# A q projection ahead of z, w1's low parts behind ol, and the second layer norm's sums on other engines

## The chip, the cores and the metric

The kernel runs on one core of one Trainium2 chip. The core has five engines, each with an instruction queue of its own that is worked off in order: TensorE (PE in the profile, with its weight loads as PEld), VectorE (DVE), ScalarE (ACT), GpSimd (POOL) and SyncE (SP), which here only issues transfers. They wait for each other through semaphores. Matrix products are written to PSUM, a small memory of banks; everything else on the chip lies in SBUF. The metric is the time of one execution on the device in microseconds, as the median of several runs.

## The reference

The block has 2048 tokens of 512 channels, in fp32. First comes linear attention with 32 heads of 16 channels, whose features are two softmaxes per head, of the projected logits and of their negative:

```python
pq = einsum("bhsd,hdf->bhsf", q, w_phi)          # q, k, v = layernorm(x) @ wqkv, by heads
phi_q = concat([softmax(pq), softmax(-pq)], -1)  # phi_k from k in the same way
kv = einsum("bhsf,bhsd->bhfd", phi_k, v)
z  = einsum("bhsf->bhf", phi_k)
num = einsum("bhqf,bhfd->bhqd", phi_q, kv)
den = einsum("bhqf,bhf->bhq", phi_q, z)[..., None] + 1e-6
h = x + (num / den) @ wo                          # heads side by side
u = gelu(einsum("bsd,sf->bdf", layernorm(h), w1) + b1)   # F = 1792, over the token axis
out = h + transpose(einsum("bdf,fs->bds", u, w2) + b2)
```

z is a sum over all tokens, so no den can be computed before the last k tile is done. The second layer norm needs the mean and the variance of every row of h.

## The kernel before

**Tiling.** The tokens are cut into 16 tiles of 128 rows. Every fp32 operand of a large product is split into a high part (rounded to fp32r by ScalarE, `whi`, `xs`, `oh`, `hs`) and a low part (the rest, by a subtraction on DVE or POOL, `wlo`, `ol`, `wol`). Each product is then three matmuls, high by high, high by low and low by high (`mm3`, L61 to L63). One projection of a tile is four such triples, twelve matmuls of 512 columns.

**Stages.** A first stage folds w_phi into the weights and computes k, v and the sums kv and zacc for all tiles (to some 144 us of the profile), with six of the q tiles in between. The main loop, `for it in range(NT + 3)`, follows (144 to 276 us). It carries a token tile through several iterations: iteration `it` transposes the features of tile it (`s_tr`), computes num of tile it-1 (`s_num`), the output product of tile it-2 (`s_wo`) and its h (`s_h`), and the normalised tile it-3 (`s_hn`). The first two columns of w1, `fill(0)` and `fill(1)`, are multiplied with finished tiles inside this loop. After it come the rest of w1 and gelu, and from about 340 us the products with w2, in which PE never stands still.

**What sets the order.** A planner orders the instructions by its own cost estimates. Between `ms.enter_context(tc.manual_schedule(...))`, behind the loop over the k tiles, and `ms.close()`, behind the main loop, the order on PE, DVE, ACT and POOL is that of the program text; so each of these engines' queues can be read off the code. SP's queue and everything behind `ms.close()` stay with the planner.

**q tiles.** `q_mm` issues the next q tile's projection into one of the two PSUM buffers of `ps_q` (tag `pu`), so tile n+2 needs the buffer of tile n. `q_logits` takes the per-head maximum and minimum on DVE, subtracts the maximum on DVE (L144), and, for tiles 6 and later, copies the logits on ACT (L146), after which the buffer is free; `negate` then forms the negative half on POOL (L159). `q_exp` is one exponential on ACT (L169). q tiles 6 to 9 are issued in the straight piece of text between the loop over k and the main loop; tile 10 in iteration 0, tiles 11 and 12 in iteration 1, where tile 11 follows num of tile 0, and so on to tile 15 in iteration 4. From iteration 5 on `fill(1)` uses the buffers of `ps_q`.

**z and den.** The last addition to zacc is DVE's (L481). Two products with a matrix of ones (L486) spread zacc to all rows, ACT copies the result to zB (L487), and POOL multiplies each q tile's exponentials with it (`s_ez`, L440). `s_den` reduces this on DVE (from L449, tile `tz`) to the weights W, and `s_pq` (L458) applies W on POOL. `wo_hi` and `wo_lo` (L426, L429) split wo on ACT and POOL, row block by row block. They stand in the same straight piece.

**The main loop's waits.** num and the transposes share one PSUM tile (`tn`, one buffer): the transposes of tile it wait for ol of tile it-1 (DVE, L553), which waits for oh (ACT, L548); num waits for the copies `pht` (ACT, L528). The output product has one buffer `po`, freed by `s_h`, whose addition (L568) reads it. `s_h` then computes the mean and the variance by bn_stats and bn_aggr and prepares two columns of `ve2`. `s_rstd` turns them into the scale and the shift on POOL (a power and a product). `s_hn` normalises on ACT and splits the tile on ACT and POOL (`hs`).

**w1.** `stream` loads two row blocks of one w1 column pair, ACT forms the high part and DVE the low part at once (`split`, L56 and L57). `fill_load` calls it at the end of an iteration. The first pairs are loaded in iteration 2, further ones in about every second iteration for both columns.

Of the kernel before, what the change touches and what calls it, by code (L numbers as in the profile page):

```python
# [17 lines left out]
P = 128  # L18
# [15 lines left out]
def block_kernel(ctx: ExitStack, tc: tile.TileContext, x, xT, wT, phic, wo, w1, b1, w2, b2,  # L34
# [10 lines left out]
    b1s = cst.tile([P, NF], F32, name="b1s")  # L45
    b2s = cst.tile([P, NT], F32, name="b2s")
    r1 = cst.tile([P, NT], F32, name="r1")
    mv2 = cst.tile([P, NT, 2], F32, name="mv2")
    r2 = cst.tile([P, NT], F32, name="r2")
    cst.tile([P, 56], F32, name="pad")  # L50
    nc.vector.memset(ones, 1.0)
    nc.vector.memset(mhalf, -0.5)

    def split(hi, lo, src, lo_engine):

        nc.scalar.activation(hi, src, AF.Copy)  # L56
        return lo_engine.tensor_sub(lo, src, hi)  # L57
# [97 lines left out]
    def negate():  # L155

        if MN:
            ev, mn = MN.pop(0)
            nc.gpsimd.tensor_sub(ev[:, :, 1], mn.unsqueeze(3).to_broadcast([P, NPR, 2, DH]), ev[:, :, 1])  # L159

    def run(*lists):

        for i in range(max(map(len, lists))):
            for ops in lists:
                if i < len(ops):
                    ops[i]()
# [192 lines left out]
    def q_mm():  # L359
        if q["mm"] < NT:  # L360
            PS[q["mm"]] = proj(q["mm"], wqh, wql, ps_q, "pu")
            q["mm"] += 1
# [65 lines left out]
    def wo_lo(j):  # L428
        nc.gpsimd.tensor_sub(wol[:, j], WO[j], woh[:, j])  # L429
# [27 lines left out]
    def s_pq(t):  # L457
        nc.gpsimd.tensor_mul(heads(EQ[t]), heads(EQ[t]), W[t].rearrange("p g c h -> p (g c h)").unsqueeze(2).to_broadcast([P, 2 * H, DH]))  # L458

    def lead(it, mm):  # L460

        if 0 <= it + 1 < NT:
            s_pq(it + 1)
        if 0 <= it + 3 < NT:
            s_ez(it + 3)
        negate()
        for _ in range(mm):
            q_mm()
        q_exp(0)
# [4 lines left out]
    k_norm(NT - 1, False)  # L474
    for j in range(KD):
        wo_hi(j)
    wo_lo(0)
    wo_lo(1)
    v_kv()
    run(q_logits(0))  # L480
    nc.vector.tensor_add(zacc, zacc, PK[NT - 1])  # L481
    negate()
    zB = big.tile([P, NG, P], F32, name="zB", tag="big")
    for g in range(2):
        pz = ps_k.tile([P, 4, P], F32, name="pk_ps")
# [2 lines left out]
    q_exp(0)  # L488
    s_ez(0)
    s_ez(1)  # L490
    wo_lo(2)
    wo_lo(3)
    q_mm()
    v_kv()
    run(s_den(0))
    run(q_logits(0))
# [54 lines left out]
    def s_ol(t):  # L551
        oh, ol, pn = OS[t]
        return [lambda: nc.vector.tensor_sub(ol, pn, oh)]  # L553
# [11 lines left out]
    def s_h(t):  # L565

        h = HT[t]
        nc.vector.tensor_add(h, PO.pop(t), h)  # L568
        nc.sync.dma_start(out[t * P:(t + 1) * P, :], h)
        st = ak.tile([P, 6], F32, name="st2")  # L570
        nc.vector.bn_stats(st, h)
        nc.vector.bn_aggr(mv2[:, t, :], st)
        VE[t] = ak.tile([P, 2], F32, name="ve2")
        nc.vector.tensor_scalar(VE[t][:, 0:1], mv2[:, t, 1:2], 1.0 + EPS, EPS * EPS, op0=ALU.mult, op1=ALU.add)
        nc.vector.tensor_scalar_mul(VE[t][:, 1:2], mv2[:, t, 0:1], -1.0)

    def s_rstd(t):
        nc.gpsimd.tensor_tensor(r2[:, t:t + 1], VE[t][:, 0:1], mhalf[:, :1], op=ALU.pow)
# [8 lines left out]
    w1v = w1.rearrange("(k p) f -> p k f", p=P)  # L587
    w2v = w2.rearrange("(k p) s -> p k s", p=P)

    def stream(src, k0, n, c0, w):  # L590

        raw = wf.tile([P, n, w], F32, name="wraw")
        wh_ = wf.tile([P, n, w], F32R, name="whi")
        wl_ = wf.tile([P, n, w], F32R, name="wlo")
        nc.sync.dma_start(raw, src[:, k0:k0 + n, c0:c0 + w])
        LO.append(split(wh_, wl_, raw, nc.vector).ins)
        return wh_, wl_

    PU, WI, LO = {}, {}, []
# [7 lines left out]
    def fill(p, pool=None):  # L607

        t = FN[p]
        FN[p] = t + 1  # L610
        if FL[p] <= t:
            fill_load(p)
        if t == 0:
            PU[p] = [pool.tile([P, D], F32, name="pu", tag="pu") for _ in range(2)]
        a, b = WI[p, t - t % 2]
        for c in range(2):
            mm3(PU[p][c], a[:, t % 2, c * P:(c + 1) * P], b[:, t % 2, c * P:(c + 1) * P],
                HN[t][:, 0], HN[t][:, 1], t == 0, t == NT - 1)

    for it in range(NT + 3):  # L620
        if 0 <= it < NT:
            s_x(it)
        if 0 <= it - 3 < NT:
            s_rstd(it - 3)
        if 0 <= it - 1 < NT:
            s_num(it - 1)
        if 0 <= it - 2 < NT:
            s_wo(it - 2)
        if it == 1:
            run(q_logits(0))  # L630
            q_mm()
        if 0 <= it < NT:
            s_tr(it)
        if it == 0:
            s_kv()
        lead(it, 1)
        den = s_den(it + 2) if it + 2 < NT else []
        run((s_ol(it - 1) if 0 <= it - 1 < NT else []) + q_logits(1) + (q_sums(0) if it > 0 else []), den)
        if it > 0:
            negate()  # L640
        if 0 <= it - 3 < NT:
            s_hn(it - 3)
        if 0 <= it - 2 < NT:
            s_h(it - 2)
        if FN[0] <= it - LAG:
            fill(0, ps_f)
        for _ in range(2):
            if q["logits"] == NT and FN[1] <= it - LAG:
                fill(1, ps_q)
        for p in range(2):  # L650
            if it >= LAG - 2 and FL[p] <= FN[p] + 1:
                fill_load(p)
    ms.close()
    a2.close()
    aq.close()
# [195 lines left out]
```

## Time and profile before

| | us |
|---|---|
| median of 3 runs | 536.01 (535.8 to 536.05) |
| profiled execution | 535.76 |
| its span, first to last instruction | 534.0 |
| PE busy | 522.6 |
| DVE busy | 393.5 |
| ACT busy | 258.6 |
| POOL busy | 236.6 |
| PE idle, 120 to 160 us | 1.69 |
| PE idle, 160 to 220 us | 2.26 |
| PE idle, 220 to 400 us | 0.0 |

A row of a timeline has the start of an instruction (or of several alike, merged, with their count) from the span's start, its duration, both in microseconds, its engine, its line, the operation, the tile written and the tiles read with their sizes, and in brackets how long its engine had been idle before it and what it waited for. A row of a group of instructions has the line, the engine, the shapes and the count, then the total busy time in us and the mean of one in ns, then the idle time in front of the group and what ended it. PE's matmuls overlap: each lasts longer than the distance to the next.

### The profile page before, as it was taken

How to read it: one execution, taken by the hardware profiler on the slowest of the kernel's cores; microseconds unless marked ns; L12 is line 12 of the kernel's file. 1: busy time of each engine (PE TensorE's matmuls, PEld its weight loads, DVE VectorE, ACT ScalarE, POOL GpSimd, SP SyncE). 2: the span in 40 equal slices, each digit the busy share in tenths (PEclk: the TensorE clock that was granted, in tenths of full speed). 3: DMA queues.
4: the chain of work that ended last, by engine and by line, in shares of the span. 5: the costliest groups of instructions: out<-in, count | busy, mean ns of one | idle time of the engine just before them, and what ended most of it. 6: DMA issues, size and time to landing. Idle time of an engine off the chain costs nothing.

```text
span 534.0 us, 9892 instructions
## 1 busy us (share of the span) xinstructions
PE 522.6 (98%) x3872; PEld 450.4 (84%) x3872; DVE 393.5 (74%) x722; ACT 258.6 (48%) x406; POOL 236.6 (44%) x184
## 2 busy tenths in 40 slices
PE   8999999998999999999999999999999999999995
PEld 7888888886876777778788888888899999999995
DVE  6993999875699989986536523835768878888774
ACT  6998844434346555544546423525443343343340
POOL 2589699878978989985435000000001101100110
PEclk9999999999999999999999999999999999999998
DMA  8534300021302233333256333533014556536631
GB/s 315 196 113 118 99 21 21 1 78 63 97 4 86 73 101 118 100 121 118 91 166 179 98 100 97 160 107 91 20 41 108 139 149 144 133 119 140 138 80 40
DMA packets 45486, 55.84 MB, mean 105 GB/s; under 512 B 3968, under 2 KB 33024, under 8 KB 45440
## 3 DMA queue, kind: packets, MB, share of 16 engines
q1 hardware_dynamic: 43136, 51.38, 30.2%
q0 software_dynamic: 2016, 3.67, 5.1%
q8 instruction: 30, 0.49, 0.4%
q10 hardware_dynamic: 288, 0.17, 0.1%
q14 instruction: 16, 0.13, 0.1%
HBM read 46.81 MB, written 8.39 MB: 103 GB/s over the span
## 4 chain that ended last, share of the span: by engine, by line
PE 91%; DVE 5%; ACT 2%; issue 1%; POOL 0%; DVEq 0%; POOLq 0%
PE py L745 26%; PE pu L61 12%; PE pu L62 12%; PE pu L63 12%; PE po L61 3%; PE pv L62 3%; PE pv L63 3%; PE pv L61 3%; PE pk_ps L61 2%; PE pk_ps L63 2%; PE pk_ps L62 2%; PE tn L526 2%; PE po L62 2%; PE po L63 2%; PE kvp L205 2%; PE tn L544 1%
## 5 line engine op out<-in xcount | busy, mean ns | idle before, releaser
L57 DVE TENSOR_TENSOR wlo<-wraw,whi 128x512 fp32r<-128x512 f32 (+1 forms) x84 | 100.3, 1204 | 69.4 <-ACT whi L56 67.9
L56 ACT ACTIVATE whi<-wraw 128x512 fp32r<-128x512 f32 (+1 forms) x84 | 81.9, 987 | 127.1 <-PE py L745 73.8
L783 POOL DMA_DIRECT2D out<-ot x14 | 12.5, 1001 | 211.3 <-DVE ot L781 211.3
L745 PE MATMUL py<-uf,whi 128*128 128x256 f32 x560 | 96.2, 283 | 0.0
L61 PE MATMUL pu<-hs,whi 128*128 128x512 f32 x224 | 87.6, 394 | 0.6 <-ACT eq L146 0.6
L62 PE MATMUL pu<-hs,whi 128*128 128x512 f32 x224 | 87.2, 389 | 0.0
L63 PE MATMUL pu<-hs,wlo 128*128 128x512 f32 x224 | 86.8, 389 | 0.0
L745 PEld LDWEIGHTS py<-uf,whi 128*128 128x128 f32 x560 | 83.3, 192 | 0.0
L745 PE MATMUL py<-uf,wlo 128*128 128x256 f32 x280 | 69.9, 283 | 0.0
L61 PEld LDWEIGHTS pu<-hs,whi 128*128 128x128 f32 x224 | 42.1, 188 | 9.5 <-ACT eq L146 1.1
L745 PEld LDWEIGHTS py<-uf,wlo 128*128 128x128 f32 x280 | 49.7, 192 | 0.0
L63 PEld LDWEIGHTS pu<-hs,wlo 128*128 128x128 f32 x224 | 42.0, 188 | 8.8
L62 PEld LDWEIGHTS pu<-hs,whi 128*128 128x128 f32 x224 | 42.1, 188 | 8.2
L528 ACT ACTIVATE pht<-tn 128x512 f32<-128x512 f32 x32 | 17.4, 596 | 49.7 <-PE tn L526 49.7
L440 POOL TENSOR_TENSOR ez<-eq,zB 128x1024 f32<-128x1024 f32 x16 | 38.4, 2406 | 0.7 <-ACT zB L487 0.7
L745 PE MATMUL py<-un,whi 128*128 128x256 f32 x224 | 38.4, 283 | 0.0
L193 POOL TENSOR_TENSOR pk<-pk,sk 128x1024 f32<-128x1024 f32 x16 | 31.1, 1944 | 9.4 <-DVE sk L192 7.6
L745 PEld LDWEIGHTS py<-un,whi 128*128 128x128 f32 x224 | 33.2, 192 | 0.1
L458 POOL TENSOR_TENSOR eq<-eq,w 128x1024 f32<-128x1024 f32 x16 | 31.1, 1942 | 3.1 <-DVE w L455 3.1
L197 POOL TENSOR_TENSOR zacc<-zacc,pk 128x1024 f32<-128x1024 f32 x13 | 31.3, 2409 | 0.6
L57 POOL TENSOR_TENSOR hs<-hn,hs 128x512 fp32r<-128x512 f32 x16 | 20.6, 1291 | 21.1 <-ACT hs L56 21.1
L61 PE MATMUL po<-woh,oh 128*128 128x512 f32 x64 | 26.6, 416 | 1.0 <-DVE h L568 1.0
(161 smaller groups left out, 1144.3 us busy)
## 6 DMA issues: line engine op xcount, KB each, us to landing
wraw<-in_w SPq DMA_DIRECT2D x112, 256.0 KB, 2.8
xraw<-in_xT SPq DMA_DIRECT2D x16, 256.0 KB, 3.1
xh<-in_x SPq DMA_DIRECT2D x16, 256.0 KB, 2.7
h<-in_x SPq DMA_DIRECT2D x16, 256.0 KB, 2.9
out<-h SPq DMA_DIRECT2D x16, 256.0 KB, 2.2
out<-ot POOLq DMA_DIRECT2D x14, 256.0 KB, 4.8
wraw<-in_wT SPq DMA_DIRECT2D x12, 256.0 KB, 4.9
wo<-in_wo SPq DMA_DIRECT2D x4, 256.0 KB, 3.8
```

The lines of the kernel that those rows point to most:

```text
L56: nc.scalar.activation(hi, src, AF.Copy)
L57: return lo_engine.tensor_sub(lo, src, hi)
L61: nc.tensor.matmul(o, ah, bh, start=first, stop=False)
L62: nc.tensor.matmul(o, ah, bl, start=False, stop=False)
L63: nc.tensor.matmul(o, al, bh, start=False, stop=last)
L193: nc.gpsimd.tensor_mul(heads(PK[t]), heads(PK[t]), sk.unsqueeze(2).to_broadcast([P, 2 * H, DH]))
L197: nc.gpsimd.tensor_add(zacc, zacc, PK[t])
L440: nc.gpsimd.tensor_mul(EZ[t], EQ[t], zB)
L458: nc.gpsimd.tensor_mul(heads(EQ[t]), heads(EQ[t]), W[t].rearrange("p g c h -> p (g c h)").unsqueeze(2).to_broadcast([P, 2 * H, DH]))
L528: nc.scalar.activation(PHT[t][:, half * 4:half * 4 + 4, :], ptr[:, half], AF.Copy)
L745: nc.tensor.matmul(o, a[x], b[:, y], start=start and i == 0, stop=stop and i == 2, skip_group_check=True)
L783: nc.gpsimd.dma_start(out[(t + i) * P:(t + i + 1) * P, :], flat(ot[:, i]), accum_op=ALU.add)
```

## The change

Five edits, in the order of the diff:

- The tile `mv2` goes and a column `eps2`, set once, comes. The pad behind them grows.
- In the straight piece in front of the main loop the projection of q tile 7 (`q_mm`) moves from behind zB's copies to in front of z's two products; zacc's last addition is made in two halves; of wo's four low parts one (instead of two) stands in front of zB, behind the negation of q tile 6 instead of in front of it, and three (instead of two) stand behind the first two `s_ez`.
- h's addition becomes a `scalar_tensor_tensor` that also gives the row's sum. bn_stats, bn_aggr and two small instructions on DVE go. In the next iteration ACT makes the negative mean, one pass of squares with their sum, and the variance column (`s_moments`), behind oh and in front of the `pht` copies.
- On POOL `s_pq` moves from `lead` to the front of `s_rstd`, which stood first in the iteration.
- w1's low parts are not subtracted at once: `stream` puts them on a list, and `flush` empties it behind ol of the next iteration (and at once where `fill` itself had to load).

```diff
-    mv2 = cst.tile([P, NT, 2], F32, name="mv2")
+    eps2 = cst.tile([P, 1], F32, name="eps2")
...
+    nc.vector.memset(eps2, EPS * EPS)
...
     def lead(it, mm):
-        if 0 <= it + 1 < NT:
-            s_pq(it + 1)
         if 0 <= it + 3 < NT:
             s_ez(it + 3)
...
-    wo_lo(0)
-    wo_lo(1)
     v_kv()
     run(q_logits(0))
-    nc.vector.tensor_add(zacc, zacc, PK[NT - 1])
+    for g in range(2):
+        nc.vector.tensor_add(zacc[:, 4 * g:4 * g + 4, :], zacc[:, 4 * g:4 * g + 4, :], PK[NT - 1][:, 4 * g:4 * g + 4, :])
     negate()
+    wo_lo(0)
+    q_mm()
     zB = big.tile([P, NG, P], F32, name="zB", tag="big")
...
     q_exp(0)
     s_ez(0)
     s_ez(1)
-    wo_lo(2)
-    wo_lo(3)
-    q_mm()
+    for j in range(1, KD):
+        wo_lo(j)
     v_kv()
...
     def s_h(t):
         h = HT[t]
-        nc.vector.tensor_add(h, PO.pop(t), h)
+        VE[t] = ak.tile([P, 4], F32, name="ve2", bufs=3)
+        nc.vector.scalar_tensor_tensor(h, PO.pop(t), 1.0, h, op0=ALU.mult, op1=ALU.add, accum_out=VE[t][:, 2:3])
         nc.sync.dma_start(out[t * P:(t + 1) * P, :], h)
-        st = ak.tile([P, 6], F32, name="st2")
-        nc.vector.bn_stats(st, h)
-        nc.vector.bn_aggr(mv2[:, t, :], st)
-        VE[t] = ak.tile([P, 2], F32, name="ve2")
-        nc.vector.tensor_scalar(VE[t][:, 0:1], mv2[:, t, 1:2], 1.0 + EPS, EPS * EPS, op0=ALU.mult, op1=ALU.add)
-        nc.vector.tensor_scalar_mul(VE[t][:, 1:2], mv2[:, t, 0:1], -1.0)
+
+    def s_moments(t):
+        junk = ak.tile([P, D], F32, name="hj", bufs=1)
+        nc.scalar.activation(VE[t][:, 1:2], VE[t][:, 2:3], AF.Copy, scale=-1.0 / D)
+        nc.scalar.activation(junk, HT[t], AF.Square, bias=VE[t][:, 1:2], accum_out=VE[t][:, 3:4])
+        nc.scalar.activation(VE[t][:, 0:1], VE[t][:, 3:4], AF.Identity, scale=(1.0 + EPS) / D, bias=eps2)
...
+    LATER = []
+
+    def flush():
+        while LATER:
+            wl_, raw, wh_ = LATER.pop(0)
+            LO.append(nc.vector.tensor_sub(wl_, raw, wh_).ins)
...
-        LO.append(split(wh_, wl_, raw, nc.vector).ins)
+        nc.scalar.activation(wh_, raw, AF.Copy)
+        LATER.append((wl_, raw, wh_))
...
         if FL[p] <= t:
             fill_load(p)
+            flush()
...
             s_x(it)
-        if 0 <= it - 3 < NT:
-            s_rstd(it - 3)
         if 0 <= it - 1 < NT:
             s_num(it - 1)
+        if 0 <= it - 3 < NT:
+            s_moments(it - 3)
         if 0 <= it - 2 < NT:
             s_wo(it - 2)
...
+        if 0 <= it + 1 < NT:
+            s_pq(it + 1)
+        if 0 <= it - 3 < NT:
+            s_rstd(it - 3)
         lead(it, 1)
         den = s_den(it + 2) if it + 2 < NT else []
-        run((s_ol(it - 1) if 0 <= it - 1 < NT else []) + q_logits(1) + (q_sums(0) if it > 0 else []), den)
+        run(s_ol(it - 1) if 0 <= it - 1 < NT else [])
+        flush()
+        run(q_logits(1) + (q_sums(0) if it > 0 else []), den)
...
+    flush()
     ms.close()
```

More of the change, by code (lines that the diff above doesn't have):

```diff
@@ L47, in block_kernel @@
     r1 = cst.tile([P, NT], F32, name="r1")
-    mv2 = cst.tile([P, NT, 2], F32, name="mv2")
+    eps2 = cst.tile([P, 1], F32, name="eps2")
     r2 = cst.tile([P, NT], F32, name="r2")
-    cst.tile([P, 56], F32, name="pad")
+    cst.tile([P, 80], F32, name="pad")
     nc.vector.memset(ones, 1.0)
     nc.vector.memset(mhalf, -0.5)
+    nc.vector.memset(eps2, EPS * EPS)
     def split(hi, lo, src, lo_engine):
@@ L161, in run @@
     def run(*lists):
-        for i in range(max(map(len, lists))):
+        for i in range(max(len(x) for x in lists)):
             for ops in lists:
```

## The prediction

> **What bounds the kernel now.** I read the page first, then the timeline of TensorE (PE) from 115 to 300 us for places where it stands still, then the timelines of GpSimd (POOL), ScalarE (ACT) and VectorE (DVE) around each. The page:
>
> ```profile
> span 534.0 us, 9892 instructions
> PE 522.6 (98%) x3872; PEld 450.4 (84%) x3872; DVE 393.5 (74%) x722; ACT 258.6 (48%) x406; POOL 236.6 (44%) x184
> PEclk9999999999999999999999999999999999999998
> ```
>
> PE is busy for 98% of the span, at full clock. So the change can win only where PE waits in the stretch that it edits. These rows bound that:
>
> ```profile
> 121.89 0.39 PE L61 MATMUL pv<-wvh,xs 128*128 128x512 f32 x1
> 124.39 0.39 PE L63 MATMUL pv<-wvh,xs 128*128 128x512 f32 x1
> 126.46 1.96 PE L486 MATMUL pk_ps<-zacc,ones 128*128 128x512 f32 x4 [1.69 <-DVE zacc L481]
> ...
> 148.27 0.67 PE L544 MATMUL tn<-pht,kvB 64*32 64x128 f32 x32
> 148.86 0.50 PE L61 MATMUL pu<-wqh,xs 128*128 128x512 f32 x1
> ...
> 171.71 0.50 PE L61 MATMUL po<-woh,oh 128*128 128x512 f32 x1 [1.03 <-DVE h L568]
> ...
> 186.82 0.50 PE L61 MATMUL pu<-hs,whi 128*128 128x512 f32 x1 [0.65 <-ACT eq L146]
> ...
> 200.38 1.06 PE L526 MATMUL tn<-ident,eq 128*128 128x128 f32 x8 [0.53 <-DVE ol L553]
> ```
>
> The twelve matmuls of one projection start at 121.89 and 124.39 for first and last: 2.50/11 = 0.227 us apart, though each lasts 0.39. So a wait costs its idle time plus 0.39 - 0.23 = 0.16: A, in front of z, 1.85; C, in front of an output product (iteration 4), about 1.1; D, in front of a w1 product (iteration 5), 0.81; E, in front of iteration 7's transposes, 0.69. All of it is 4.5 us, under 1%.
>
> **The q tile in front of z.** q tile 7 takes 12 x 0.227 = 2.73 us and needs nothing late. It starts at 124.39 + 0.23 = 124.62 and ends at 127.34: wait A is filled, and PE is 1.85 us ahead behind z. But z starts at 127.34 instead of 126.46, 0.88 later, and zB with it. The sum for z, in two halves, is no limit: even at its old pace it ended at 126.4. Who waits for zB is POOL:
>
> ```profile
> 129.13 4.77 POOL L440 TENSOR_TENSOR ez<-eq,zB 128x1024 f32<-128x1024 f32 x2 [0.68 <-ACT zB L487]
> 133.85 2.54 POOL L429 TENSOR_TENSOR wol<-wo,woh 128x512 fp32r<-128x512 f32 x2
> ...
> 145.85 1.08 POOL L159 TENSOR_TENSOR eq<-mn,eq 128x512 f32<-128x512 f32 x1
> 149.00 1.94 POOL L458 TENSOR_TENSOR eq<-eq,w 128x1024 f32<-128x1024 f32 x1 [2.07 <-DVE w L455]
> ```
>
> From 129.13 to 146.93 POOL runs ten instructions without a gap, the last the negation of q tile 8. The change puts one more of wo's low parts into this row (three behind the ez pair instead of two: 2.54/2 = 1.27). The time that POOL is spared in front of z is lost, as it waits there for zB. So the negation ends 0.88 + 1.27 = 2.15 us later. Behind it:
>
> ```profile
> 139.34 1.15 ACT L169 ACTIVATE eq<-eq,r 128x1024 f32<-128x1024 f32 x1 [2.74 <-POOL eq L159]
> 146.96 1.16 ACT L169 ACTIVATE eq<-eq,r 128x1024 f32<-128x1024 f32 x1 [0.23 <-POOL eq L159]
> 148.02 0.57 ACT L146 ACTIVATE eq<-pu 128x512 f32<-128x512 f32 x1
> ```
>
> The exponential of tile 8 waits for that negation already (0.23). Behind it in ACT's queue stands the copy of q tile 9's logits, ending at 148.59, which frees the PSUM buffer of q tile 11: ps_q has two, and 11 follows 9. Tile 11 started at 148.86, just behind the num product, so it had at most 0.27 to spare; wait D shows 0.05 from such a copy's end (186.77) to the product. With the copy at 148.59 + 2.15 = 150.74 tile 11 starts at 150.79: **+1.93 us against before**, with no PE work left undone or done in advance. The 1.85 is not saved; it becomes part of 1.85 + 1.93 = 3.8 us of waiting, of which some 1.3 falls ahead of the last kv product (exponential 7 waits for POOL too, 2.74 in the row above, and v's last copy queues behind it) and 2.5 ahead of tile 11. After it POOL idles again (2.07 at 149.00), so the loss stays at 1.93. Below: 1.85 less, if the chain on POOL did not hold; above: 2.15.
>
> **h's sum and squares.** DVE loses bn_stats and its three small followers and h's addition takes the fused form:
>
> ```profile
> 163.16 0.69 DVE L571 BATCH_NORM_STATS2 st<-h 128x6 f32<-128x512 f32 x1
> L568 DVE TENSOR_TENSOR h<-po,h 128x512 f32<-128x512 f32 x16 | 10.9, 684 | 6.1 <-PE po L63 6.1
> L781 DVE SCALAR_TENSOR_TENSOR ot<-py,b2s,u 128x512 f32<-128x512 f32 x7 | 5.2, 748 | 0.0
> L113 ACT ACTIVATE sqj<-xh,st 128x512 f32<-128x512 f32 x16 | 11.5, 721 | 0.3
> L113 ACT ACTIVATION_READ_ACCUMULATOR sqj<-xh,st 128x1 f32 x16 | 3.0, 191 | 0.0
> 184.16 1.09 ACT L528 ACTIVATE pht<-tn 128x512 f32<-128x512 f32 x2 [3.15 <-PE tn L526]
> ```
>
> Saved on DVE: 163.16 to 164.24 (below), 1.08 us a tile. Added: 0.06 by the fused form (748 - 684); writing out its sum is in no row, 0 to 0.19 by ACT's accumulator read; I take 0. ACT pays 0.72 + 0.19 and two instructions on one column (about 0.2 each), 1.3 us, between oh and the pht copies, where it waits 3.15 for PE: nothing. If that cover went, 1.3 an iteration. POOL's rstd, now behind pq, would wait for ACT with ez and the negation behind it; pq's 1.94 covers that.
>
> **w1's low parts behind ol.** Wait C first, in rows of ACT, DVE and POOL:
>
> ```profile
> 163.54 0.61 ACT L548 ACTIVATE oh<-tn 128x512 fp32r<-128x512 f32 x1
> 164.24 1.28 DVE L57 TENSOR_TENSOR wlo<-wraw,whi 128x512 fp32r<-128x512 f32 x2
> 165.44 0.68 DVE L553 TENSOR_TENSOR ol<-tn,oh 128x512 fp32r<-128x512 f32 x1
> 166.04 1.21 DVE L449 TENSOR_REDUCE tz<-ez 128x64 f32<-128x1024 f32 x1
> 170.97 0.68 DVE L568 TENSOR_TENSOR h<-po,h 128x512 f32<-128x512 f32 x1
> 162.70 1.06 POOL L159 TENSOR_TENSOR eq<-mn,eq 128x512 f32<-128x512 f32 x1 [1.07 <-ACT eq L146]
> 165.55 1.93 POOL L458 TENSOR_TENSOR eq<-eq,w 128x1024 f32<-128x1024 f32 x1
> ```
>
> Before: statistics, two wlo, ol, then 4.93 us from tz (166.04) to h (170.97), and PE 0.74 later. After: ol cannot use the 1.08 saved, for it waits for oh, which ACT gives behind two whi copies at 164.15. In PE's new time (+1.93): oh 166.08, ol to 166.72, two wlo at 0.6 each to 167.92, h at 172.85, PE at 173.59, against 171.71 + 1.93 = 173.64. C stays; the short wait ahead of it at 166 goes into it. But the wlo now fall on POOL's pq, moved up to 163.76 + 1.93 = 165.69 and running to 167.6. What that does:
>
> ```profile
> 179.70 1.29 POOL L57 TENSOR_TENSOR hs<-hn,hs 128x512 fp32r<-128x512 f32 x1 [0.30 <-ACT hs L56]
> 180.18 1.36 DVE L57 TENSOR_TENSOR wlo<-wraw,whi 128x512 fp32r<-128x512 f32 x1
> ```
>
> Beside POOL's subtraction wlo took 1.36 instead of 0.68 and ended 0.55 behind it (181.54 against 180.99). The same beside pq: first wlo to 168.15, second 168.75, h at 173.68, PE at 174.42: **+0.78**, with the fused form +0.84. No row has wlo beside pq (one input of which is a small broadcast), so 0 to 0.84; I take the upper end, as the hs row is the nearest. The Trainium skill (SBUF — State Buffer, section "Who interferes with whom") says that a VectorE instruction with two SBUF inputs contends with any GpSimd instruction that reads SBUF, and that the loser blocks fully; the hs row agrees. By that rule the sum has the 0.84 and D's 0.55 below; without it neither.
>
> D: q tile 15's logits copy frees the buffer.
>
> ```profile
> 180.41 0.60 ACT L548 ACTIVATE oh<-tn 128x512 fp32r<-128x512 f32 x1 [0.26 <-PE tn L544]
> 182.06 1.20 DVE L449 TENSOR_REDUCE tz<-ez 128x64 f32<-128x1024 f32 x1
> 184.60 0.68 DVE L144 TENSOR_TENSOR eq<-pu,mx 128x512 f32<-128x512 f32 x1
> 186.18 0.59 ACT L146 ACTIVATE eq<-pu 128x512 f32<-128x512 f32 x1
> ```
>
> At +2.77 (1.93 + 0.84): oh ends at 183.78, ol at 184.4; pq starts behind hs at 183.76 and holds wlo until 185.7 + 0.55 = 186.25; the shift, 3.22 behind tz's start, ends at 189.47; ACT was ready to copy at 188.95. **+0.5**, or 0 without the blocking.
>
> ```profile
> 197.66 1.98 DVE L57 TENSOR_TENSOR wlo<-wraw,whi 128x512 fp32r<-128x512 f32 x2 [0.84 <-ACT whi L56]
> ```
>
> E: ol stood behind these two (with 0.84 of waiting for whi). Now it goes as soon as oh is there: **-0.69**. Next late would be oh, ready with about 0.3 to spare. Queue SP's loads of w1 wait for wraw a little longer, four buffers deep: nothing.
>
> **Sum.** 1.93 + 0.84 + 0.5 - 0.69 = +2.6. The profiled execution took 535.76 (span 534.0), 0.25 below the median: 538.4 us; from the median 538.6; I say 538.5. Both ends of the blocking give 537.1 to 538.4.
>
> **Rivals.**
> 1. *The blocking costs nothing and DVE's relief counts* (pq leaves wlo alone, and ol comes earlier than I think). 1.93 - 0.69 = +1.2, less up to 1.1 if C also goes: 535.9 to 537.0. For it: no row shows pq against wlo. Against: C's chain starts at oh, which the change does not speed up.
> 2. *Faster: POOL does not hold PE.* If wo's three low parts run while POOL waits for zB, instead of between ez and pq, the row to the negation of tile 8 is 17.8 - 2.54 = 15.26 from 130.01, ends at 145.3, 1.7 earlier than before, and PE keeps the 1.85: -1.85 - 0.69 = -2.5, or -1.2 with the blocking: 533.2 to 534.6. It decides when that negation ends by 145.3 or so. For it: they need only woh, done long before. Against: before's POOL kept them behind the ez pair, at 133.85.
> 3. *The clock falls in the new wait.* At the kernel's start PE ran a slow stretch:
>
> ```profile
> L286 PE MATMUL pk_ps<-ones 128*128 128x128 f32 x18 | 4.2, 430 | 1.1 <-DVE mhalf L52 1.1
> ```
>
> These matmuls stand 0.23 apart (4.2/18); twice as fast they would take 2.1 less. If the wait ahead of tile 11 is long enough, the same is paid again: 540.5. For it: 3.8 us of waiting within 9. Against: A's 1.85 left the clock at 9 in every slice. The Trainium skill (TensorE: Matmul & The Clock Gate, Part 1) names an idle window of about 3.4 us; by it 2.5 us would not do and one wait of 3.8 would.
>
> **How the numbers follow.** Main case, with or without half of the blocking (537.1 to 539.2): 0.64. Rival 1: 0.16. Rival 2: 0.12. Rival 3: 0.08. A difference under 0.2% (1.07 us) can't be told from none here, so faster 0.12, same 0.15, slower 0.73. The range 535.8 to 540.3 leaves out rival 2 and the end of rival 3; the main case's own is 537.0 to 539.2.
>
> **What would show it.** Right: no idle ahead of z, z 0.9 later; exponential 8 waits some 4 us for POOL; PE waits for ACT's copy ahead of q tile 11 by some 2.5 us and for v's copy ahead of the last kv products; wlo beside pq near 1.3 us; PE straight through iteration 7; 16 statistics gone from DVE; ACT's squares ahead of pht without delaying it. Wrong: tile 11 right behind num, or a wait for ACT's moments ahead of hn on POOL and PE, or a new order in the planned parts before 115 and after 275 us, where PE has nothing to gain.

## The result and the profile after

The changed kernel takes 542.8 us (median of four runs, 542.31 to 543.4) against 535.99 us before, measured beside it: a ratio of 1.0127, 95% interval 1.0112 to 1.0142. It is slower, as forecast, but by 6.8 us and not by 2.5, and it lies above the range of 535.8 to 540.3. The profiled execution took 543.4 us, with a span of 541.6.

The page of the changed kernel:

```profile
span 541.6 us, 9889 instructions
PE 524.0 (97%) x3872; PEld 451.8 (83%) x3872; DVE 376.8 (70%) x676; ACT 277.6 (51%) x470; POOL 233.2 (43%) x184
PEclk9999999999989999999999999999999999999999
```

VectorE (DVE) has 16.7 us less to do and TensorE (PE) the same 3872 matmuls, yet the span is 7.7 us longer. One slice of the clock's row has an 8. So the time lies in new idle places of PE and in one stretch at a lower clock. These are PE's rows in the changed kernel that show a wait, with the start of q tile 6's projection (the last piece of work ahead of everything that the change touches) and the last matmul ahead of z:

```profile
119.36 0.50 PE L62 MATMUL pu<-wqh,xs 128*128 128x512 f32 x1
...
127.42 0.40 PE L64 MATMUL pu<-wqh,xs 128*128 128x512 f32 x1
127.65 0.59 PE L486 MATMUL pk_ps<-zacc,ones 128*128 128x512 f32 x1
...
143.57 0.65 PE L206 MATMUL kvp<-pk,vs 128*32 128x64 f32 x32 [1.31 <-ACT vs L185]
...
150.97 0.80 PE L62 MATMUL pu<-wqh,xs 128*128 128x512 f32 x1 [2.15 <-ACT eq L147]
...
167.27 0.50 PE L62 MATMUL po<-woh,oh 128*128 128x512 f32 x1 [0.34 <-DVE h L568]
176.27 0.50 PE L62 MATMUL po<-woh,oh 128*128 128x512 f32 x1 [1.75 <-DVE h L568]
...
191.71 0.50 PE L62 MATMUL pu<-hs,whi 128*128 128x512 f32 x1 [0.95 <-ACT eq L147]
...
210.78 0.50 PE L62 MATMUL po<-woh,oh 128*128 128x512 f32 x1 [1.84 <-DVE h L568]
...
225.93 0.50 PE L62 MATMUL po<-woh,oh 128*128 128x512 f32 x1 [0.77 <-DVE h L568]
241.07 0.50 PE L62 MATMUL po<-woh,oh 128*128 128x512 f32 x1 [0.77 <-DVE h L568]
```

In the kernel before, q tile 6 starts earlier:

```profile
119.04 0.50 PE L61 MATMUL pu<-wqh,xs 128*128 128x512 f32 x1
```

So 0.32 us of the span's 7.66 (541.62 against 533.96, first start to last end) arose ahead of the change: in other kernels below with the same first stage this start wanders between 119.0 and 119.7. I therefore count from q tile 6's start: 414.92 us before, 422.26 after, +7.34.

Where these 7.34 arise, by the start of the same matmul in both traces, less the 0.32:

| place | start before, after | lost there |
|---|---|---|
| q tile 11 waits for its PSUM buffer | 148.86, 150.97 | 1.79 |
| its first matmuls at the lower clock (to the transposes of iteration 1) | 151.72, 155.41 | 1.58 |
| output product, iteration 3 | 163.18, 167.27 | 0.40 |
| output product, iteration 4 (C) | 171.71, 176.27 | 0.47 |
| w1 product, iteration 5 (D), up to iteration 6's transposes | 192.54, 197.43 | 0.33 |
| transposes of iteration 7 (E) | 200.38, 204.58 | -0.69 |
| output product, iteration 8 | 204.75, 210.78 | 1.83 |
| output product, iteration 10 | 219.06, 225.93 | 0.84 |
| output product, iteration 12 | 233.36, 241.07 | 0.84 |

The rest, -0.05, is spread to the end. Two blocks carry the loss: q tile 11 with its clock (3.37) and the output products in iterations 8, 10 and 12 (3.51).

The chain ahead of q tile 11, on GpSimd (POOL) and ScalarE (ACT) of the changed kernel:

```profile
130.25 4.75 POOL L441 TENSOR_TENSOR ez<-eq,zB 128x1024 f32<-128x1024 f32 x2 [1.25 <-ACT zB L487]
134.96 3.80 POOL L430 TENSOR_TENSOR wol<-wo,woh 128x512 fp32r<-128x512 f32 x3
...
148.19 1.07 POOL L160 TENSOR_TENSOR eq<-mn,eq 128x512 f32<-128x512 f32 x1
149.29 1.15 ACT L170 ACTIVATE eq<-eq,r 128x1024 f32<-128x1024 f32 x1 [2.64 <-POOL eq L160]
150.34 0.57 ACT L147 ACTIVATE eq<-pu 128x512 f32<-128x512 f32 x1
```

Negation of tile 8 to 149.26, exponential, copy of tile 9's logits to 150.91, q tile 11 at 150.97: link by link the row that the prediction gave. Behind it q tile 11's matmuls start 0.43 us apart, and 0.23 apart again from 154.49 on:

```profile
151.99 0.63 PE L64 MATMUL pu<-wqh,xs 128*128 128x512 f32 x1
152.42 0.63 PE L62 MATMUL pu<-wqh,xs 128*128 128x512 f32 x1
...
154.49 0.40 PE L64 MATMUL pu<-wqh,xs 128*128 128x512 f32 x1
154.72 0.40 PE L62 MATMUL pu<-wqh,xs 128*128 128x512 f32 x1
```

The windows of the changed kernel (busy time of PE, PEld, DVE, ACT, POOL, then PE's granted clock, the share and rate of the DMA) show the same stretch as a clock of 0.96, where before it was 1.00:

```profile
115.00:160.00 45.00, 41.54 (x414) 32.51 (x414) 28.47 (x54) 17.52 (x28) 33.82 (x20) 0.96 0.23 72
```

The second block, iteration 7, on DVE and POOL of the changed kernel:

```profile
203.54 0.69 DVE L552 TENSOR_TENSOR ol<-tn,oh 128x512 fp32r<-128x512 f32 x1 [2.38 <-ACT oh L547]
204.15 2.27 DVE L596 TENSOR_TENSOR wlo<-wraw,whi 128x512 fp32r<-128x512 f32 x2
...
210.04 0.68 DVE L568 SCALAR_TENSOR_TENSOR h<-po,h 128x512 f32<-128x512 f32 x1
210.64 0.08 DVE L568 DVE_READ_ACCUMULATOR h<-po,h 128x1 f32 x1
...
203.32 1.94 POOL L459 TENSOR_TENSOR eq<-eq,w 128x1024 f32<-128x1024 f32 x1
205.22 1.00 POOL L579 TENSOR_TENSOR r<-ve,mhalf 128x1 f32<-128x1 f32 x1
```

and the same place before, DVE and then PE:

```profile
203.99 0.68 DVE L568 TENSOR_TENSOR h<-po,h 128x512 f32<-128x512 f32 x1
...
204.75 0.50 PE L61 MATMUL po<-woh,oh 128*128 128x512 f32 x1
```

Before, h ended at 204.67 and the product that needs the buffer `po` started at 204.75: there was 0.08 us to spare at most (where the product did wait, at 171.71, it started 0.06 us after h's end). After, two low parts stand between ol and h. They start at 204.15 and the next instruction starts at 206.34: 2.19 us on a chain with no slack. POOL's pq overlaps the first and its power the second; the power, 0.55 elsewhere, takes 1.00.

### The profile page after: what moved, and what is told of

Same layout as the page of the kernel before. It is cut to its first block, busy times and chain, and to the rows that moved or that the text cites. A ratio compares the mean times of both kernels' runs of the same rounds, so it can differ in the third digit from the quotient of the medians.

```text
span 541.6 us, 9889 instructions
## 1 busy us (share of the span) xinstructions
PE 524.0 (97%) x3872; PEld 451.8 (83%) x3872; DVE 376.8 (70%) x676; ACT 277.6 (51%) x470; POOL 233.2 (43%) x184
## 4 chain that ended last, share of the span: by engine, by line
PE 82%; DVE 8%; ACT 4%; POOL 3%; DMA 1%; issue 1%; SPq 0%; DVEq 0%; ACTq 0%; POOLq 0%
PE py L762 26%; PE pu L62 10%; PE pu L63 10%; PE pu L64 10%; PE pk_ps L62 2%; PE pv L63 2%; PE pk_ps L63 2%; PE pk_ps L64 2%; PE pv L64 2%; PE pv L62 2%; PE po L62 2%; DVE wlo L596 2%; PE po L63 2%; PE po L64 2%; POOL ez L441 2%; PE tn L525 2%
## 5 line engine op out<-in xcount | busy, mean ns | idle before, releaser
L57 ACT ACTIVATE whi<-wraw 128x1792 fp32r<-128x1792 f32 x28 | 47.7, 1704 | 77.9 <-PE py L762 70.5
L596 DVE TENSOR_TENSOR wlo<-wraw,whi 128x512 fp32r<-128x512 f32 x56 | 45.3, 820 | 48.8 <-ACT whi L604 44.0
L58 DVE TENSOR_TENSOR wlo<-wraw,whi 128x1792 fp32r<-128x1792 f32 x28 | 56.6, 2022 | 18.3 <-ACT whi L57 18.1
L604 ACT ACTIVATE whi<-wraw 128x512 fp32r<-128x512 f32 x56 | 34.4, 626 | 45.5 <-PE pu L63 41.4
```

Source lines behind the costliest of these rows:

```text
L596: LO.append(nc.vector.tensor_sub(wl_, raw, wh_).ins)
L604: nc.scalar.activation(wh_, raw, AF.Copy)
```

## The experiments

Each kernel is made from the changed kernel or the one before by the edit shown. I started with two theories. One: the loss lies in the straight piece (POOL's chain and the clock behind it). Two: it lies in the loop, where w1's low parts meet POOL's reads of SBUF. The rival to each was that the other carries it.

**The straight piece alone.** The kernel before, with only the second edit of the change.

```diff
-    wo_lo(0)
-    wo_lo(1)
     v_kv()
     run(q_logits(0))
...
     negate()
+    wo_lo(0)
+    q_mm()
...
-    wo_lo(2)
-    wo_lo(3)
-    q_mm()
+    for j in range(1, KD):
+        wo_lo(j)
```

> Of the change only the straight piece in front of the main loop: q tile 7 ahead of z, zacc's addition in halves, one of wo's low parts later. Theory 1 (POOL's row of instructions behind zB holds q tile 11, and the wait of over 2 us in front of it lowers TensorE's clock for a few matmuls): q tile 11 starts some 2 us later than before, its matmuls stand 0.43 instead of 0.23 apart for about seven of them, and all of it stays: +3.3 to +3.8 us, 539.3 to 539.8. Rival (the straight piece only moves waiting about, the loss is made in the main loop): 534 to 536.5.

Measured: 539.55 us, ratio 1.0067 (1.0052 to 1.0082), +3.7. In its trace q tile 11 starts at 150.62 behind 2.13 us of idle time, and the next transposes are 4.45 us behind that start where they were 2.86 before: 1.6 us at the lower clock here as well. So the first block is this edit's alone.

**The loop alone.** The changed kernel with the old straight piece (the diff above, reversed).

> The changed kernel with the straight piece as before; the edits of the main loop alone. Theory 1: the loop's edits lose the rest, +3.5 to +4.3 us (539.5 to 540.3), by output products that wait for h in iterations 4, 8, 10 and 12, and there is no wait in front of q tile 11. Rival: all of the 6.8 stays, 542 to 543, or nothing does, 535.5 to 536.5.

Measured: 542.85 us, ratio 1.0128 (1.0113 to 1.0143): +7.0, as dear as the whole change, and a miss for what I expected. From q tile 6 its profiled span is 420.82, +5.90 over before; the straight piece alone has +3.44. Together 9.34, not 7.34. Of the 2.00 between them 0.35 is z's wait, which is 2.04 here and 1.69 before; 1.57 is one stretch of slow clock that is counted twice: without the wait at q tile 11, the clock fell in this execution at the wait of 1.77 us in iteration 4 (173.57 to the transposes at 178.02: 4.45 us, where the whole change has 176.27 to 179.15, 2.88). Each of the two profiles has one such stretch, and so has that of the whole change. The waits in iterations 8, 10 and 12 are there unchanged (1.84, 0.77, 0.77).

**One part of the loop at a time.** First the kernel before with w1's low parts behind ol and nothing else:

```diff
-        LO.append(split(wh_, wl_, raw, nc.vector).ins)
+        nc.scalar.activation(wh_, raw, AF.Copy)
+        LATER.append((wl_, raw, wh_))
...
+        run(s_ol(it - 1) if 0 <= it - 1 < NT else [])
+        flush()
```

> Before with w1's low parts behind the next ol, statistics and POOL's order as before. Theory 2 (the low parts stand between oh and h, stretched by POOL's work, so that h comes after PE wants its buffer): waits of 0.8 to 2 us in front of the output product in iterations 8, 10 and 12, some 3 us in all, less 0.7 for iteration 7: 538 to 540. Rival (it is the squares on ScalarE, or pq's new place, that make h late): 535 to 536.

Then the kernel before with the sum, the squares and pq ahead of the scale and shift, and the low parts left where they were (in both kernels DVE's list behind ol is split in two as in the change):

```diff
-        nc.vector.tensor_add(h, PO.pop(t), h)
+        nc.vector.scalar_tensor_tensor(h, PO.pop(t), 1.0, h, op0=ALU.mult, op1=ALU.add, accum_out=VE[t][:, 2:3])
...
+            s_moments(it - 3)
...
+            s_pq(it + 1)
             s_rstd(it - 3)
```

> Before with h's sum in its addition, the squares on ScalarE and pq ahead of rstd; w1's low parts at once, as before. Theory 2: DVE has 1 us less to do between two tiles, nothing waits for ScalarE, so 0.5 to 1.3 us faster: 534.7 to 535.5. Rival (squares on ScalarE make something late): 537 to 539.

Measured: 553.9 us, ratio 1.0341 (1.0315 to 1.0366), and 546.28 us, ratio 1.0195 (1.0178 to 1.0211). Each half alone is dearer than the two together (542.85), by 11 and 3.4 us; their profiles have stretches at the lower clock too. DVE, POOL and PE of the kernel with only the late low parts, iterations 7 and 8:

```profile
199.91 5.25 DVE L595 TENSOR_TENSOR wlo<-wraw,whi 128x512 fp32r<-128x512 f32 x2
...
199.85 1.94 POOL L458 TENSOR_TENSOR eq<-eq,w 128x1024 f32<-128x1024 f32 x1
201.75 2.85 POOL L440 TENSOR_TENSOR ez<-eq,zB 128x1024 f32<-128x1024 f32 x1
...
209.52 0.79 PE L61 MATMUL po<-woh,oh 128*128 128x512 f32 x1 [4.53 <-DVE h L568]
```

Here pq and ez follow each other on POOL without a gap. The low parts and these two instructions take turns: the first low part ends 0.55 us behind pq (202.34 against 201.79), ez, which came up beside it, takes 2.85 where it is 2.40 elsewhere, and the second low part ends 0.56 us behind ez (205.16 against 204.60). Together the two take 5.25 us. In the change the scale and shift stand between pq and ez and let DVE in: 2.19. The kernel with only the new sums:

```profile
200.17 3.72 DVE L58 TENSOR_TENSOR wlo<-wraw,whi 128x512 fp32r<-128x512 f32 x2 [2.16 <-ACT whi L57]
...
200.95 2.39 POOL L459 TENSOR_TENSOR eq<-eq,w 128x1024 f32<-128x1024 f32 x1
...
204.64 0.63 PE L525 MATMUL tn<-ident,eq 128*128 128x128 f32 x4 [2.27 <-POOL ve L580]
```

Its low parts stand in front of ol and take 3.72 us, and the wait falls in front of the transposes. The profile names POOL's `ve` as what came last; ol, which the transposes need for the buffer `tn`, follows the low parts at 203.81 and ends at 204.49, 0.15 us ahead of them. Both are late by the same meeting of pq and the low parts; which of the two held PE this run does not separate.

So it is not the moving of the low parts as such, but which POOL instruction they meet. The next two kernels test that from two sides.

**The low parts without a second SBUF operand.** The changed kernel, with the flush behind ol subtracting a PSUM tile (q's sums, zeroed at the start) instead of the high part. It leaves out w1's low parts, so its products with w1 are of other numbers, but as many.

```diff
+            if alone:
+                LO.append(nc.vector.tensor_sub(wl_, raw, sums.rearrange(...)).ins)
...
-        flush()
+        flush(True)
```

> The changed kernel, but inside the main loop w1's low parts are computed from the loaded block and a PSUM tile (q's sums, zeroed at the start) instead of the block and its high part, so that the subtraction reads one SBUF operand; w1's low parts are left out thereby, and their product is that of other numbers. Theory 2 (beside POOL's work a subtraction with two SBUF operands waits for a whole POOL instruction, and that makes h late): two of them take 1.3 us instead of 2.0 to 2.3, the waits for h in iterations 10 and 12 go, that in 8 halves, that in 4 loses 0.7: 538.5 to 540. Rival (DVE has too much to do between oh and h in any case): 542 to 543.

**pq behind the scale and shift again.**

```diff
-        if 0 <= it + 1 < NT:
-            s_pq(it + 1)
         if 0 <= it - 3 < NT:
             s_rstd(it - 3)
+        if 0 <= it + 1 < NT:
+            s_pq(it + 1)
```

> The changed kernel with rstd ahead of pq on POOL again, so that pq and ez follow each other without the short power between them, beside w1's low parts. Theory 2: the second low part then waits for ez too, two take some 5 us instead of 2.2, and the waits for h in iterations 8, 10 and 12 grow by 2 to 3 us each: 548 to 552. Rival (pq's place is of no matter, or rstd waits for ScalarE and leaves POOL idle beside the low parts): 540 to 543.

Measured: 539.12 us (ratio 1.0058, 1.0042 to 1.0075) and 538.98 us (1.0055, 1.004 to 1.007). Both take 3.7 to 3.8 us off the changed kernel. The first, DVE:

```profile
202.44 1.27 DVE L598 TENSOR_TENSOR wlo<-wraw,smq 128x512 fp32r<-128x512 f32 x2
```

As many instructions over as many elements at the same place beside the same pq, with one operand in PSUM, take 1.27 instead of 2.27. That shows the contention. The second kernel I had expected to be far slower (the low parts beside pq and ez, as in the kernel above), and it went the other way. Its DVE and POOL:

```profile
202.96 1.28 DVE L596 TENSOR_TENSOR wlo<-wraw,whi 128x512 fp32r<-128x512 f32 x2
...
203.66 0.99 POOL L579 TENSOR_TENSOR r<-ve,mhalf 128x1 f32<-128x1 f32 x1 [1.49 <-ACT ve L576]
...
204.88 1.94 POOL L459 TENSOR_TENSOR eq<-eq,w 128x1024 f32<-128x1024 f32 x1
```

The power waits 1.49 us for ACT's variance, and holds pq and ez back behind it. In that gap the low parts pass. Before the new sums, the power did not wait there, which is why the same order cost 553.9 in the kernel with only the late low parts. The waits in iterations 10 and 12 are gone in both kernels; in iteration 8 half of the 1.83 stays (from the transposes of iteration 7 at 203.39 to the product at 208.61 it is 5.22 us in the second kernel, 4.37 before: 0.85), as the low parts' own 1.2 us still stand ahead of h.

**The clock in the wait.** The changed kernel with ten products of ones ahead of q tile 11, so that PE does not stand still there.

```diff
             run(q_logits(0))
+            keep = ps_f.tile([P, P], F32, name="pu", tag="pu")
+            for _ in range(10):
+                nc.tensor.matmul(keep, ones, ones, start=True, stop=True)
             q_mm()
```

> The changed kernel with ten small products of ones, whose result nobody reads, in front of q tile 11, to keep TensorE busy while it waits there. Theory 1 (the idle time in front of tile 11 lowers the clock, and seven matmuls at 0.43 instead of 0.23 apart are the price): the wait stays, the matmuls behind it stand 0.23 apart, 1.2 to 1.6 us less than the changed kernel: 541.2 to 541.6. Rival (tile 11 is slow for another reason): 542.5 to 543.2.

Measured: 543.34 us, ratio 1.0132 (1.0117 to 1.0147): no gain. q tile 11 ran at full speed (its start to the next transposes is 2.84 us), but in iteration 4 the clock fell at the wait of 1.76 us, which had been harmless in the changed kernel's profile. The windows:

```profile
160.00:185.00 25.00, 22.90 (x193) 17.90 (x192) 19.91 (x43) 15.83 (x30) 20.16 (x16) 0.93 0.21 69
```

So the slow stretch does not belong to one place. Nor does every such wait bring it: in the profile of the kernel whose low parts read a PSUM tile, PE waits 2.15 us ahead of q tile 11 and the clock stays at 1.00 from 115 to 245 us.

**The exponentials off the chain.** The changed kernel with exponential 7 behind v's last copy and the copy of tile 8's logits, and exponential 8 in iteration 1, behind the copies that free the buffers.

```diff
     negate()
-    q_exp(0)
     s_ez(2)
     q_mm()
     v_kv()
     run(s_den(1))
     run(q_logits(0))
+    q_exp(0)
...
-        q_exp(0)
+        if it:
+            q_exp(0)
+        if it == 1:
+            q_exp(0)
```

> The changed kernel with two exponentials on ScalarE moved: that of q tile 7 behind v's last copy and the logits copy of tile 8, that of tile 8 from iteration 0 to iteration 1, behind the copy of tile 9's logits and oh. Nothing on POOL is changed. Theory 1 (tile 11 waits for a PSUM buffer whose release stands in ScalarE's queue behind an exponential that waits for POOL): no wait ahead of the last kv products, tile 11 starts at about 147 us, and iteration 1 begins at about 150 instead of 155.4: 5 to 5.8 us less than the changed kernel, 537 to 538. Rival (POOL's products hold the loop by other ways, pq above all): iteration 1 begins at 152 to 154, 540 to 541.5.

Measured: 540.13 us, ratio 1.0073 (1.0055 to 1.0091). ACT's copy of tile 9's logits, and the waits that PE then has:

```profile
146.30 0.60 ACT L147 ACTIVATE eq<-pu 128x512 f32<-128x512 f32 x1 [1.46 <-DVE eq L145]
...
162.99 0.50 PE L62 MATMUL po<-woh,oh 128*128 128x512 f32 x1 [1.29 <-DVE h L571]
...
205.78 0.51 PE L62 MATMUL po<-woh,oh 128*128 128x512 f32 x1 [1.83 <-DVE h L571]
```

The mechanism is as described: the copy waits for DVE only, q tile 11 starts at 146.96 and iteration 1 at 149.84 instead of 155.41, 5.3 us earlier once the 0.30 at q tile 6 is taken off. But iteration 3's output product then waits 1.29 us for h, and in this execution the clock fell at 205.78 (that product to the next takes 8.74 us, where 7.15 is the pace). Of the 5.3 us, 2.7 remained.

**wo's low parts all ahead of zB**, in the changed kernel (the second rival of the prediction):

```diff
+    wo_lo(0)
+    wo_lo(1)
     v_kv()
...
     negate()
-    wo_lo(0)
+    wo_lo(2)
+    wo_lo(3)
     q_mm()
...
-    for j in range(1, KD):
-        wo_lo(j)
```

> The changed kernel with all four of wo's low parts in front of zB on POOL, two ahead of the negation of q tile 6 and two behind it. Theory 1 (three low parts between ez and pq hold the negation of q tile 8, and with it tile 11): POOL's row behind zB is 3.8 us shorter, no wait in front of tile 11, full clock, and the wait in front of z stays filled: 5 to 5.6 us less than the changed kernel, 537.2 to 538. Rival (z's 0.9 us alone hold tile 11): 540 to 541.

Measured: 541.92 us, ratio 1.0103 (1.0086 to 1.0121). DVE, POOL and PE:

```profile
125.07 3.46 DVE L481 TENSOR_TENSOR zacc<-zacc,pk 128x512 f32<-128x512 f32 x2 [0.41 <-POOL pk L194]
...
131.89 4.74 POOL L441 TENSOR_TENSOR ez<-eq,zB 128x1024 f32<-128x1024 f32 x2
...
149.82 0.50 PE L62 MATMUL pu<-wqh,xs 128*128 128x512 f32 x1 [1.73 <-ACT eq L147]
```

Now zacc's two halves meet wo's low parts and take 3.46 us (1.29 in the changed kernel), and POOL begins ez at 131.89 instead of 130.25. Of the 3.8 us taken out of POOL's chain, 1.15 came through to q tile 11 (1.50 from q tile 6's start). The gain in time, 0.9 us, is hardly clear of the noise: the two intervals overlap, and in this profile the clock fell behind iteration 8's wait instead (0.94 from 185 to 215 us).

**The straight piece with the later exponentials, loop of before.**

```diff
-    wo_lo(0)
-    wo_lo(1)
     v_kv()
...
     negate()
+    wo_lo(0)
+    q_mm()
...
-    q_exp(0)
     s_ez(2)
     q_mm()
     v_kv()
     run(s_den(1))
     run(q_logits(0))
+    q_exp(0)
```

> Before with the straight piece of the change and the exponentials of tiles 7 and 8 later; the loop as before. Theory 1: the 1.85 us in front of z are won and kept: 533.8 to 534.8. Rival (POOL holds the loop anyway): 536 to 538.

Measured: 536.08 us (ten runs), ratio 0.9998 (0.9989 to 1.0008): no difference. z no longer waits, q tile 11 no longer waits; in iteration 3 the output product waits 1.11 us for h (at 164.02), where it did not before, and C, D and E stay. What was won ahead of the loop was given back within three iterations.

**The low parts behind h instead of behind ol**, first with the later exponentials and with pq behind the scale and shift, then with the old straight piece and pq behind the scale and shift:

```diff
         run(s_ol(it - 1) if 0 <= it - 1 < NT else [])
-        flush()
...
             s_h(it - 2)
+        flush()
```

> The two together: the changed kernel with the exponentials of tiles 7 and 8 later, rstd ahead of pq and the low parts behind h. If both theories hold, 1.85 us are won in front of the loop and 1 to 2 in it: 532 to 533.5, faster than before. If one falls, 534 to 538.

> The straight piece as before; in the main loop h's sum and ScalarE's squares as in the changed kernel, rstd ahead of pq again, and w1's low parts behind h instead of behind ol, beside POOL's hs. Theory 2 (between oh and h there must be no low part, and beside one of them POOL should have one long instruction at most): no wait for h in iterations 4, 8, 10 and 12, none for ol in 7; the wait in front of a w1 product in iteration 5 stays: 1 to 2 us less than before, 534 to 535.2. Rival (behind h the low parts hold the next ol instead, as with the statistics gone alone): 538 to 545.

Measured: 537.92 us (1.0033, 1.002 to 1.0047) for the first, 540.26 us (1.0084, 1.0066 to 1.0102) for the second. The low parts no longer delay h there. But in iteration 6 the w1 product itself waits for its low part, 2.0 us in either (at 196.08 and 199.66). Each profile has a fall of the clock behind that wait (0.83 from 195 to 205 us, 0.83 from 200 to 210 us), and that of the second kernel another behind z's wait of 2.04 us (0.93 from 120 to 145 us). This is the other end of the room: behind ol they delay h, behind h they are late for their own product.

**Both repairs, low parts behind ol.** The later exponentials and pq behind the scale and shift, and nothing else against the changed kernel.

```diff
-        if 0 <= it + 1 < NT:
-            s_pq(it + 1)
         if 0 <= it - 3 < NT:
             s_rstd(it - 3)
+        if 0 <= it + 1 < NT:
+            s_pq(it + 1)
...
-        q_exp(0)
+        if it:
+            q_exp(0)
+        if it == 1:
+            q_exp(0)
```

> The change with its two dear places undone together: exponentials 7 and 8 later in ScalarE's queue (as in the run where that was done alone, 540.1 us) and the scale and shift ahead of the weighting with W on GpSimd (as in the run where that was done alone, 539.0 us), the low parts staying behind ol. Theory: the two losses are separate and their savings against the changed kernel's 542.8 us add, 2.7 + 3.8 = 6.5: 536.3 us, the time of before within 0.2%. Rival: after the first 2.7 us the loop's next wait (for h in iterations 1 to 4, on GpSimd's queue) takes up most of it, as it did alone: 537.5 to 538.5 us. If the theory holds and the slow clock goes too, 535.3 us, faster than both kernels.

Measured: 535.07 us (11 runs, 534.6 to 535.61) against 536.08 of before, ratio 0.9981 (0.9972 to 0.999). It is 7.7 us faster than the changed kernel, where 2.7 + 3.8 = 6.5 would be the plain sum, and 1.0 us faster than before: a difference just under the 0.2% that I called measurable, but its interval leaves out no change. Its waits:

```profile
163.09 0.50 PE L62 MATMUL po<-woh,oh 128*128 128x512 f32 x1 [1.29 <-DVE h L571]
...
170.63 0.50 PE L62 MATMUL po<-woh,oh 128*128 128x512 f32 x1 [0.30 <-DVE h L571]
...
185.77 0.50 PE L62 MATMUL pu<-hs,whi 128*128 128x512 f32 x1 [0.64 <-ACT eq L147]
203.89 0.50 PE L62 MATMUL po<-woh,oh 128*128 128x512 f32 x1 [0.86 <-DVE h L571]
```

No wait is as long as 1.5 us, and its granted clock is 1.00 in every window from 115 to 245 us. That is the likely source of the 1.2 us beyond the plain sum: in the profiles of the two single repairs one long wait was left (at q tile 11, 2.15 us, in the one, in iteration 8, 1.83 us, in the other) and the clock fell at it (0.96 from 115 to 160 us, 0.94 from 185 to 215 us). That no loss is left with both places undone is shown, and so is that each repair alone leaves a part of it; that the 1.2 is the clock rests on these profiles alone.

## Why the prediction was right in sign and wrong in size

**z and POOL's chain: right.** z starts 0.87 us later without any wait (0.88 predicted, after the 0.32), and q tile 11 1.79 us later (1.93 predicted). That the wait saved at z would come back in front of q tile 11, split over v's copy (1.31 ahead of the last kv product) and tile 9's copy (2.15), is what the trace shows. Exponential 8 waits 2.64 us for POOL, not "some 4"; it is exponential 7 that waits 3.98.

**C, D and E: right in their sum, in part by luck.** Iterations 3 and 4 lose 0.40 + 0.47 = 0.87, where 0.84 was predicted, all of it at C and by the blocking. D's place loses 0.33 (0.5 predicted), E wins 0.69 (0.69). The blocking beside pq, which no row had shown, exists: two low parts there take 2.02 to 2.27 us instead of 1.28, and with one operand in PSUM 1.27. At C it costs about what was predicted: from iteration 3's output product to iteration 4's it is 9.00 us in the changed kernel and 8.25 in the one whose low parts read a PSUM tile, 0.75 apart (0.78 predicted). The first rival, that it costs nothing, is out. The Trainium skill (SBUF — State Buffer, "Who interferes with whom") says that a VectorE instruction with two SBUF inputs contends with GpSimd's reads and that one with at most one, outside the two-port modes, does not; 2.27 and 1.27 beside the same pq agree. They bear out the blocking for one operand shape at one place; what an instruction meets there is decided by the order on POOL.

But the 0.40 in iteration 3 is no blocking, and the prediction has no term for it. PE's wait there is in the kernel with the PSUM operand too (0.34), and in each half of the loop alone (0.33 and 0.34), but not in the straight piece alone. What these kernels share is an order on DVE: to let the flush in, the edit splits one interleaved list in two, and the first step of den (`tz`), which stood ahead of the next q tile's maximum (`mx`), now stands behind it. Iteration 1 before, and in the changed kernel:

```profile
151.16 1.21 DVE L449 TENSOR_REDUCE tz<-ez 128x64 f32<-128x1024 f32 x1
152.29 0.68 DVE L151 TENSOR_REDUCE mx<-pu 128x32 f32<-128x512 f32 x1
...
155.61 0.69 DVE L152 TENSOR_REDUCE mx<-pu 128x32 f32<-128x512 f32 x1 [3.48 <-PE pu L64]
156.22 1.21 DVE L450 TENSOR_REDUCE tz<-ez 128x64 f32<-128x1024 f32 x1
```

mx waits for PE, and tz, the rest of den, the next ol and h queue up behind it. That this order makes the 0.40 is read from such rows; no run changes it alone.

**The statistics: right.** DVE's 16.7 us saved shortens none of PE's waits, and the sum written out by h's addition costs 0.08.

**The step that failed: what is late after E.** The prediction says "Next late would be oh, ready with about 0.3 to spare" and then sets everything behind iteration 7 to nothing. That term was not small but missing: the output products of iterations 8, 10 and 12 wait for h, 1.83 + 0.84 + 0.84 = 3.51 us, half of the loss. The low parts had been moved from in front of ol to behind it. In front of ol they delay the transposes; behind ol they delay h, and h frees the buffer for the next iteration's output product. In iteration 7 h ended 0.08 us ahead of that product. I had checked the chain from tz to h where PE already waited (C), but not where PE did not wait, which is where slack has to be read off rather than assumed. The two rows at 203.99 and 204.75 of the kernel before would have shown it. About half of iteration 8's share is the contention and half the low parts' own time.

**The rival that came true on top.** The third rival (the clock falls in the new wait) had a chance of 0.08 and a price of 2.1 us; it happened, at 1.58 us in the profiled execution. It is not the same in every execution: the four runs of the changed kernel took 542.31 and 542.39 at a mean clock of 0.999 and 543.2 and 543.4 at 0.996 and 0.995, so that a fall is worth some 1.0 us between whole runs. I had argued against it that A's 1.85 (1.69 idle) left the clock alone; 2.15 us of idle time does not always. The window of about 3.4 us that the Trainium skill names (TensorE: Matmul & The Clock Gate, Part 1) was no safe bound: the fall came behind single waits of 1.76 to 2.27 us of idle time, too. The Trainium skill also says there that the window runs free of the kernel, which fits that the same wait costs it in one execution and not in another; no run here shows the window itself.

**The second rival** (POOL does not hold PE) fell: the low parts stood between ez and pq (134.96), and with all of them moved ahead of zB PE still waits 1.73 us ahead of q tile 11, as zacc and zB then come later. What freed q tile 11 was to take the exponentials out of ACT's queue ahead of the copies that release the buffers.

## What to carry to other kernels

Before work is moved within an in-order queue, look up the next consumer behind its new place in every iteration, and its slack in the trace, above all where nothing waits today: slack of 0.08 us looks like no wait. Splitting a list of instructions in two to let something in moves the order of the rest, too. For a VectorE instruction with two SBUF operands, ask which GpSimd instruction runs beside it and what follows that one without a gap; here the same two subtractions took 1.28, 2.2, 3.7 or 5.25 us by that alone. In a queue, put the copies that free a buffer ahead of work that waits for a slow engine.

## What the hardware showed that I had not expected

- POOL's instructions are drawn out too when they meet VectorE's two-operand subtractions: the power on one column takes 0.99 to 1.00 us instead of 0.55, pq 2.39 instead of 1.94, ez 2.85 instead of 2.40. In these rows the instruction that is drawn out is the one that came up later, and in a run of such instructions the two engines pay in turn.
- TensorE's clock falls behind waits of 1.76 to 2.27 us of idle time in some executions and not in others (2.15 brought it in the changed kernel, not in the kernel with the PSUM operand; 1.84 in iteration 8 in the kernel with wo's low parts ahead of zB, not in the changed kernel), and the place changes from kernel to kernel: q tile 11, iteration 4, or iteration 8. In the traces from 115 us on no wait of up to 1.75 us brought it. Each fall costs about 1.6 us in a trace: seven or so matmuls 0.43 us apart instead of 0.23. Most profiles of kernels with several such waits show one fall, and removing the first of the waits (the ten products of ones) won nothing; why it comes at one and not at another is open.
